# Banded attention and a mixture of experts on one core: transposes first in a step, four copies, one buffer less for h, and other work kept out of second products

## The chip, the core and the metric

The kernel runs on one core of a Trainium2 chip, as one program. The metric is the device time of one execution in microseconds (us), as the median of several runs. Before the change it is 854.83 us (three runs, 854.17 to 855.73).

## The reference

Two stages. The first is attention with a window, over 4 sequences of 576 positions and 8 heads of 64 numbers; the second sends each of the 4 · 576 = 2304 rows through all four experts and adds their outputs with normalised weights.

```python
scores = scale * np.matmul(q, k.transpose(0, 1, 3, 2))
mask_plain = (rel >= 0) & (rel < window)
mask_dil = (rel >= 0) & (rel < window * dilation) & (rel % dilation == 0)
...
attn = np.exp(scores - max); attn = attn / (attn.sum(-1) + 1e-09)
x = (attn @ v) as rows of B * S, columns of H * D        # 2304 x 512
p = domain_probs / (domain_probs.sum(-1, keepdims=True) + 1e-09)
for e in range(E):                                       # 4 experts, F = 1024
    h = np.maximum(x @ w1[e], 0.0)
    out += p[:, e:e + 1] * (h @ w2[e])
```

## The kernel before

**Precision.** Every operand of an expert's product is split in a high and a low part (ScalarE copies the high part, L113; VectorE or GpSimd subtracts it to get the low part, L116), and each product is three matmuls: high·high, low·high, high·low.

**Attention** is 48 groups of three query blocks for a pair of heads, in 25 steps of two groups (the first two steps have one). Loop pass n works on several steps at once: it issues the q·k matmuls (`s_qk`, bank `sc`, L264) and mask and maximum (`s_max`, L278, VectorE) of step n; subtraction (`s_sub`, L294, GpSimd) and exponential (`s_exp`, L302, ScalarE) of step n−1; the row sums (`s_sum`, L310, L311, VectorE) and the scaling by their inverse (`s_norm`, L317, GpSimd) of step n−2; the transposes (`s_tr`, L329, bank `pt`), with their copies to `pts` (L336 on ScalarE, L334 on VectorE), of step n−3; and the products with v (`s_av`, L349, bank `po`), with their copies into the raw x (`xr`, L365, ScalarE), of step n−4. `stages` (L371) gives the order within a pass. `sc`, `pt` and `po` share a ring of four PSUM banks. q and k come by SyncE's queue (L245, L246); v of the first two sequences is issued by ScalarE's (L252), of the others by SyncE's.

**The experts** run in visits (u, m): 256 of F's columns (u) against a block of 768 tokens (m). A visit's first product (`mm1_a`, `mm1_b`) uses a seven-product scheme after Strassen: products of six matmuls into bank x or y, and sums of them that make h. In `mm1_b` the order is S2·T2, S1·T1, S3·T3, S4·B22, A22·T4. After S1·T1 ScalarE copies y to `s5`; after S3·T3 VectorE adds x to it (L439); A22·T4 then writes x again, so it waits for that sum, with S4·B22's matmuls between. After S4·B22 VectorE adds `u2` (L443). `mm2` is the second product, two halves of three tiles, 18 matmuls a half (L480), each tile added into `acc` by VectorE (L488). The next visit's `mm1_a` (with its sum, L423) stands around the second product's halves.

**Prepared work.** Splits of weights and of x (`x_part`: low parts on GpSimd for the first half of a block, on VectorE for the second) and sums of x (`x_sums`, L203, VectorE, four of them a half block) lie in two lists, `queue` and `later`; x of blocks 1 and 2 lies in `later`. After each yield of the experts the main loop takes one piece of `queue`, and, if `queue` is short, one of `later`. `need` runs a piece to its end where it must be ready.

**The start.** In passes 0 to 9 there are only attention and dummy matmuls (`wt`, L680) on TensorE, and the fetches of the first weights: `fetch_w1(0)` in pass 3, `fetch_w2(0)` and the row weights `pw` (L737) in pass 4, `fetch_w1(1)` in pass 7. The first product comes in pass 10 (START); from pass 15 (OPEN) twelve yields of the experts go between two attention steps.

Of the kernel before, what the change touches and what calls it, by code (L numbers as in the profile page):

```python
# [8 lines left out]
F32 = mybir.dt.float32  # L9
# [7 lines left out]
KB = QB + WINDOW  # L17
GB = 3
# [24 lines left out]
def kernel(  # L43
# [12 lines left out]
    _, which = band_masks(qT.shape[3])  # L56
    B, NP, _, S = qT.shape
    NT, DM = out.shape
    E, _, F = w1.shape
# [160 lines left out]
    def attention(ap, xrp, pa):  # L220
# [14 lines left out]
        st = {}  # L235
# [11 lines left out]
            qk_t[b, p, gi] = (q_s, k_s)  # L247

        def load_v(b, p, gi):
            v_s = ap.tile([KB, 2, GB, 64], F32, tag="v", name="v_s", bufs=6)  # L250
            queue = nc.scalar if b < 2 else nc.sync
            queue.dma_start(out=v_s, in_=vw[b, p][:, :, gi * GB:(gi + 1) * GB, :])  # L252
            v_t[b, p, gi] = v_s
# [69 lines left out]
        def s_tr(n, gs):  # L323
            sm = st[n]
            outs = []
            for k in range(len(gs)):
                pt = pa.tile([128, 512], F32, tag="pa", name="pt")
                for i in range(GB):
                    nc.tensor.transpose(  # L329
                        pt[:KB, i * 128:(i + 1) * 128], sm[:, k * GB + i, :KB], ident  # L330
                    )
                ts_ = ap.tile([KB, GB * 128], F32, tag="pts", name="pts", bufs=2)
                if k and gs[k][0] > 1:
                    nc.vector.tensor_copy(ts_, pt[:KB, :GB * 128])  # L334
                else:
                    nc.scalar.activation(out=ts_, in_=pt[:KB, :GB * 128], func=AF.Copy)  # L336
                outs.append(ts_)
            st[n] = outs
# [28 lines left out]
        def load_masks():  # L367
            nc.sync.dma_start(out=mask, in_=masks)


        stages = (  # L371
            (s_sub, 1), (s_sum, 2), (s_av, 4), (s_tr, 3), (s_norm, 2), (s_exp, 1),
            (s_qk, 0), (s_max, 0),
        )
        return chunk, load_masks, load_qk, load_v, stages
# [2 lines left out]
    def product(bank, u, a, m, b_, first, last=True):  # L378
        (ah, al), (bh, bl) = a_op[u, a], x_op(m, b_)
        for k in range(2):  # L380
            for i, (w, x) in enumerate(((ah, bh), (al, bh), (ah, bl))):
                nc.tensor.matmul(  # L382
                    bank, w[:, k], x[:, k],
                    start=(first and k == 0 and i == 0), stop=(last and k == 1 and i == 2),
                    skip_group_check=True,
                )
# [3 lines left out]
    st = {}  # L390

    def bank(n):
        return pools["m1"].tile([128, 512], F32, tag=n, name=f"m1{n}")[:, :TH]

    def tmp(n):
        return fp.tile([128, TH], F32, tag=n, name=n)
# [30 lines left out]

    def mm1_b(k):
        u, m = k
        x, u2, s5 = st.pop(k), tmp("u2"), tmp("s5")  # L430
        product(x, u, "S2", m, "T2", False)
        nc.scalar.activation(out=u2, in_=x, func=AF.Copy)  # L432
        yield
        y = bank("y")
        product(y, u, "S1", m, "T1", True)
        nc.scalar.activation(out=s5, in_=y, func=AF.Copy)
        yield
        product(x, u, "S3", m, "T3", False)
        nc.vector.tensor_tensor(out=s5, in0=x, in1=s5, op=ALU.add)  # L439
        yield  # L440
        product(y, u, "S4", m, "B22", False)
        h_hi(k, "22", s5)
        nc.vector.tensor_tensor(out=u2, in0=y, in1=u2, op=ALU.add)  # L443
        h_lo(k, "22", s5)
        h_out(k, "12", u2)
        yield
        product(x, u, "A22", m, "T4", False)
        h_out(k, "21", x)
        yield
# [13 lines left out]
    def mm2(k, first, last, half):  # L463
        u, m = k
        e = u // FPE % E
        if first and m not in acc_t:
            if m == NBL - 1:
                pools["late"]()
            acc_t[m] = pools["acc"].tile([128, TB // 128, DM], F32, name=f"acc_{m}")
        for i in range(TH // 128):  # L470
            at = half * (TH // 128) + i
            tt = m * (TB // 128) + at
            acc = acc_t[m][:, at, :]
            po = pools["m2"].tile([128, 512], F32, tag="m2", name="m2")

            cs = range(2) if half == 0 else (1, 0)
            for n, (c, low) in enumerate([(c, low) for low in range(2) for c in cs]):
                h = h_t[k, f"{c + 1}{half + 1}"][low][:, i * 128:(i + 1) * 128]
                for x, w in enumerate(w2_op[u, c][:2 - low]):
                    nc.tensor.matmul(  # L480
                        po, h, w, start=(n == 0 and x == 0), stop=(n == 3)
                    )
            if first:
                nc.vector.tensor_scalar(
                    out=acc, in0=po, scalar1=pn[:, tt, e:e + 1], scalar2=None, op0=ALU.mult
                )
            else:
                nc.vector.scalar_tensor_tensor(  # L488
                    out=acc, in0=po, scalar=pn[:, tt, e:e + 1], in1=acc,
                    op0=ALU.mult, op1=ALU.add,  # L490
                )
            if last:
                nc.sync.dma_start(out=out[tt * 128:(tt + 1) * 128, :], in_=acc)
            yield


    visits = [(u, 0) for u in range(1, NU)]
# [68 lines left out]
    queue = []  # L566
    later = []

    def step(of=None):
        of = queue if of is None else of  # L570
        while of:
            if next(of[0][1], 0) != 0:
                return
            of.pop(0)
# [15 lines left out]
    with tc.manual_schedule():  # L590
# [11 lines left out]
        ap = early.enter_context(tc.tile_pool(name="attn", bufs=2, side="right"))  # L602
# [99 lines left out]
        flat = [g for s in steps for g in s]  # L702
        first_x = []
        qk_done = av_done = qk_next = v_next = 0

        dummies(18)
        ffn = experts(begin)
        for n in range(len(steps) + LAG):
            while qk_next < min(qk_done + min(6, 3 + n), len(flat)):
                load_qk(*flat[qk_next])  # L710
                if qk_next == 0:
                    load_masks()
                qk_next += 1
            while v_next < min(av_done + 6, qk_done + 2, len(flat)):
                load_v(*flat[v_next])
                v_next += 1
            for stage, lag in stages:
                if 0 <= n - lag < len(steps):
                    stage(n - lag, steps[n - lag])
            if n < len(steps):  # L720
                qk_done += len(steps[n])
            if n >= LAG:
                av_done += len(steps[n - LAG])
            for i, names in when.get(n, ()):
                for name in names:
                    of = first_x if i < 2 else later
                    if name is None or name == "T2":
                        prepare(x_sums, i, of=of)
                    if name is not None:
                        prepare(x_part, i, name.upper(), of=of)  # L730
            queue[:0] = first_x
            first_x.clear()
            if n == 3:
                fetch_w1(0)
            if n == 4:
                fetch_w2(0)
                nc.sync.dma_start(out=pw, in_=probs.rearrange("(t p) e -> p t e", p=128))  # L737
            if n == 5:
                prepare(w1_split, 0)
            if n == 7:  # L740
                prepare(w2_late, 0)
                fetch_w1(1)
            if n == START + 1:
                weigh()
                prepare(w1_split, 1)
                prepare(w1_sums, 1)
            if n == OPEN - 1:
                prepare(w2_late, 1)
            if n == START + 2:
                fetch_w2(1)  # L750
            if n == OPEN:
                fetch_w1(2)
            if n == OPEN:
                gate.add("open")
            if n < START:
                dummies(4 if n < 4 else 1)
                step()
                if n > 4:
                    step()
                    step()  # L760
                continue
            for _ in range(PACE if "open" in gate else 2):
                if next(ffn) == "idle":
                    dummies(2)
                    for _ in range(3):
                        step()
                    break
                step()
                if len(queue) > 8:
                    step()  # L770
                elif later and len(queue) < 5:
                    step(later)
        gate.add("over")
        for _ in ffn:
            step()
            if len(queue) > 6:
                step()
            step(later)


# [53 lines left out]
```

## Time and profile before

| | before |
|---|---|
| median of three runs | 854.83 us |
| the profiled execution | 850.82 us |
| its span on the core | 849.0 us |
| TensorE busy | 828.1 us (98%) |
| VectorE, ScalarE, GpSimd busy | 499.9, 327.6, 419.1 us |
| granted TensorE clock, mean | 0.994 |
| bytes moved by DMA | 56.77 MB |

The span is the time between the first and the last instruction of the core, the execution's time has some 1.8 us more around it. Busy shares are means over the whole span. "Granted clock" is the share of the full 2.4 GHz that TensorE was given; near 0.5 is its lower level, 1.2 GHz. In rows of the timeline the first two numbers are start and duration in us, and a bracket at the end gives the idle time before the instruction and what ended it; a row with x3 groups three instructions.

### The profile page before, as it was taken

Reading aid. Unit: us, or ns where it says so; the run is one execution under the profiler, and the core shown is the slowest. Engines: PE = TensorE matmul, PEld = TensorE weight load, DVE = VectorE, ACT = ScalarE, POOL = GpSimd, SP = SyncE. Lnnn points to the kernel's source line nnn. Section 1 sums busy time; section 2 is a strip of 40 time slices with the busy share of each in tenths; the row PEclk is TensorE's granted clock in tenths of the full one; section 3 lists DMA queues with packets and bytes.
Section 4 is the critical chain, followed back from the end, with each engine's and each line's share of the span. In section 5 each row is a group of like instructions: output and inputs, shape, how many; then the busy total and the mean of one; then the engine's idle time right before and its main releaser. Section 6 shows DMA issues by size and latency. Waiting matters only on the chain.

```text
span 849.0 us, 13445 instructions
## 1 busy us (share of the span) xinstructions
PE 828.1 (98%) x5090; PEld 732.1 (86%) x5090; DVE 499.9 (59%) x1027; ACT 327.6 (39%) x772; POOL 419.1 (49%) x484
## 2 busy tenths in 40 slices
PE   8798999999999999999999999999999999999998
PEld 5577788887898888899899898898998998988986
DVE  4777766669555568655545545555555455455554
ACT  3555454445454355533233233242242242232321
POOL 4677987677676678931432332342341342242210
PEclk9999999999999999999999999999999999999999
DMA  8762322332221222310100100101101001010003
GB/s 234 218 184 73 128 85 84 108 120 64 78 90 51 57 71 72 124 51 26 50 25 25 51 26 26 50 25 38 37 26 50 26 25 49 26 35 17 1 26 124
DMA packets 54528, 56.77 MB, mean 67 GB/s; under 512 B 5952, under 2 KB 43840, under 8 KB 54464
## 3 DMA queue, kind: packets, MB, share of 16 engines
q1 hardware_dynamic: 49472, 52.38, 19.9%
q10 hardware_dynamic: 4992, 3.54, 1.5%
q8 instruction: 40, 0.66, 0.3%
q14 instruction: 24, 0.20, 0.1%
HBM read 51.19 MB, written 4.72 MB: 66 GB/s over the span
## 4 chain that ended last, share of the span: by engine, by line
PE 92%; DVE 3%; DMA 1%; ACT 1%; POOL 1%; issue 1%; SPq 0%; ACTq 0%; POOLq 0%; DVEq 0%
PE m L480 45%; PE m1x L382 24%; PE m1y L382 17%; PE po L349 2%; PE sc L264 2%; PE pt L329 2%; DMA q_s<-qT 1%; PE wt L680 1%; DVE acc L488 1%; DMA k_s<-kT 1%; DVE xl_T L116 1%; DVE hl L406 0%; ACT hh L400 0%; DVE xr L203 0%; DVE s L423 0%
## 5 line engine op out<-in xcount | busy, mean ns | idle before, releaser
L488 DVE SCALAR_TENSOR_TENSOR acc<-m,pn,acc 128x512 f32<-128x512 f32 x270 | 201.9, 749 | 130.9 <-PE m L480 130.7
L480 PE MATMUL m<-w2h,hh 128*128 128x512 f32 x576 | 226.9, 394 | 3.9 <-DVE acc L488 3.2
L480 PE MATMUL m<-w2l,hh 128*128 128x512 f32 x576 | 225.4, 391 | 0.0
L116 POOL TENSOR_TENSOR g2l<-r,g2h 128x256 fp32r<-128x256 f32 x124 | 93.0, 775 | 239.7 <-PE m L480 212.2
L480 PE MATMUL m<-w2h,hl 128*128 128x512 f32 x576 | 178.5, 391 | 0.0
L400 ACT ACTIVATE hh<-s 128x384 fp32r<-128x384 f32 x94 | 49.4, 526 | 248.3 <-DVE s L423 197.8
L480 PEld LDWEIGHTS m<-w2h,hh 128*128 128x128 f32 x576 | 108.1, 188 | 26.8 <-DVE acc L488 6.1
L480 PEld LDWEIGHTS m<-w2h,hl 128*128 128x128 f32 x576 | 108.1, 188 | 24.0 <-DVE hl L406 0.3
L480 PEld LDWEIGHTS m<-w2l,hh 128*128 128x128 f32 x576 | 108.2, 188 | 20.1
L116 POOL TENSOR_TENSOR w2l<-r,w2h 128x512 fp32r<-128x512 f32 x62 | 80.6, 1320 | 45.4 <-ACT w2h L113 45.0
L116 POOL TENSOR_TENSOR g1l<-r,g1h 128x256 fp32r<-128x256 f32 x93 | 68.5, 752 | 66.9 <-ACT g1h L113 66.9
L439 DVE TENSOR_TENSOR s<-m1x,s 128x384 f32<-128x384 f32 x47 | 26.2, 557 | 103.0 <-PE m1x L382 101.3
L432 ACT ACTIVATE u<-m1x 128x384 f32<-128x384 f32 x47 | 23.1, 492 | 144.4 <-PE m1x L382 144.4
L406 DVE SCALAR_TENSOR_TENSOR hl<-s,hh 128x384 fp32r<-128x384 f32 x94 | 60.2, 640 | 28.4 <-ACT hh L400 28.4
L382 PE MATMUL m1x<-xh_T,g2h 128*128 128x384 f32 x156 | 53.1, 340 | 1.8 <-DVE s L423 1.8
L382 PE MATMUL m1x<-xl_T,g2h 128*128 128x384 f32 x156 | 52.9, 339 | 0.0
L382 PE MATMUL m1x<-xh_T,g2l 128*128 128x384 f32 x156 | 52.7, 338 | 0.0
L113 ACT ACTIVATE g2h<-r 128x256 fp32r<-128x256 f32 x125 | 43.4, 405 | 4.4 <-POOL r L145 4.4
L382 PE MATMUL m1y<-xl_B,g2h 128*128 128x384 f32 x128 | 43.0, 336 | 0.0
L382 PE MATMUL m1y<-xh_B,g2h 128*128 128x384 f32 x128 | 43.0, 336 | 0.0
L382 PE MATMUL m1y<-xh_B,g2l 128*128 128x384 f32 x128 | 42.9, 335 | 0.0
L278 DVE CUSTOM_DVE_ANT_0 sm<-sc,mask 128x96 f32<-128x96 f32 x144 | 27.8, 254 | 18.8 <-PE sc L264 17.4
(92 smaller groups left out, 1542.3 us busy)
## 6 DMA issues: line engine op xcount, KB each, us to landing
r<-w SPq DMA_DIRECT2D x64, 512.0 KB, 3.5
k_s<-kT SPq DMA_DIRECT2D x48, 112.0 KB, 3.3
q_s<-qT SPq DMA_DIRECT2D x48, 96.0 KB, 3.4
out<-acc SPq DMA_DIRECT2D x18, 256.0 KB, 2.0
v_s<-vw ACTq DMA_DIRECT2D x24, 144.0 KB, 4.1
v_s<-vw SPq DMA_DIRECT2D x24, 144.0 KB, 3.2
mask<-masks SPq DMA_DIRECT2D x1, 288.0 KB, 4.6
pw<-probs SPq DMA_DIRECT2D x1, 36.0 KB, 5.9
```

Of the source, the lines that this page charges most:

```text
L113: nc.scalar.activation(out=hi, in_=src, func=AF.Copy)
L116: lo_eng.tensor_tensor(out=lo, in0=src, in1=hi.bitcast(F32), op=ALU.subtract)
L264: nc.tensor.matmul(banks[swap][o, i * KB:(i + 1) * KB], q_s[h, c0:c0 + QB], k_s[h, c0:c0 + KB], start=True, stop=True, skip_group_check=True,)
L278: nc.vector.tensor_tensor_reduce(out=sm[:, k * GB + i, :KB], in0=banks[k][:, i * KB:(i + 1) * KB], in1=mask[:, which[blk if p < NP // 2 el ...
L329: nc.tensor.transpose(pt[:KB, i * 128:(i + 1) * 128], sm[:, k * GB + i, :KB], ident)
L382: nc.tensor.matmul(bank, w[:, k], x[:, k], start=(first and k == 0 and i == 0), stop=(last and k == 1 and i == 2), skip_group_check=True,)
L400: nc.scalar.activation(out=hi, in_=src, func=AF.Relu)
L406: nc.vector.scalar_tensor_tensor(out=lo, in0=src, scalar=0.0, in1=hi.bitcast(F32), op0=ALU.max, op1=ALU.subtract)
L432: nc.scalar.activation(out=u2, in_=x, func=AF.Copy)
L439: nc.vector.tensor_tensor(out=s5, in0=x, in1=s5, op=ALU.add)
L480: nc.tensor.matmul(po, h, w, start=(n == 0 and x == 0), stop=(n == 3))
L488: nc.vector.scalar_tensor_tensor(out=acc, in0=po, scalar=pn[:, tt, e:e + 1], in1=acc, op0=ALU.mult, op1=ALU.add,)
```

## The change

1. In a pass `s_tr` comes before `s_av`, and `pts` has four buffers instead of two.
2. `s5` takes the buffer of `s1` (tag "s1") instead of its own; `v_s` has five buffers instead of six.
3. Pieces of `later` are taken only after yields of the first products (`mm2` now yields "acc"), and with fewer than 8 pieces in `queue` instead of fewer than 5.
4. q and k are loaded six groups ahead from the first pass on, instead of 3 + n at first.
5. `fetch_w2(0)` and `pw` move from pass 4 to pass 6, `w2_late(0)` and `fetch_w1(1)` from pass 7 to pass 8.

```diff
--- before.py
+++ after.py
@@ -247,7 +247,7 @@
             qk_t[b, p, gi] = (q_s, k_s)
 
         def load_v(b, p, gi):
-            v_s = ap.tile([KB, 2, GB, 64], F32, tag="v", name="v_s", bufs=6)
+            v_s = ap.tile([KB, 2, GB, 64], F32, tag="v", name="v_s", bufs=5)
             queue = nc.scalar if b < 2 else nc.sync
             queue.dma_start(out=v_s, in_=vw[b, p][:, :, gi * GB:(gi + 1) * GB, :])
             v_t[b, p, gi] = v_s
@@ -329,7 +329,7 @@
                     nc.tensor.transpose(
                         pt[:KB, i * 128:(i + 1) * 128], sm[:, k * GB + i, :KB], ident
                     )
-                ts_ = ap.tile([KB, GB * 128], F32, tag="pts", name="pts", bufs=2)
+                ts_ = ap.tile([KB, GB * 128], F32, tag="pts", name="pts", bufs=4)
                 if k and gs[k][0] > 1:
                     nc.vector.tensor_copy(ts_, pt[:KB, :GB * 128])
                 else:
@@ -369,7 +369,7 @@
 
 
         stages = (
-            (s_sub, 1), (s_sum, 2), (s_av, 4), (s_tr, 3), (s_norm, 2), (s_exp, 1),
+            (s_sub, 1), (s_sum, 2), (s_tr, 3), (s_av, 4), (s_norm, 2), (s_exp, 1),
             (s_qk, 0), (s_max, 0),
         )
         return chunk, load_masks, load_qk, load_v, stages
@@ -427,7 +427,7 @@
 
     def mm1_b(k):
         u, m = k
-        x, u2, s5 = st.pop(k), tmp("u2"), tmp("s5")
+        x, u2, s5 = st.pop(k), tmp("u2"), tmp("s1")
         product(x, u, "S2", m, "T2", False)
         nc.scalar.activation(out=u2, in_=x, func=AF.Copy)
         yield
@@ -491,7 +491,7 @@
                 )
             if last:
                 nc.sync.dma_start(out=out[tt * 128:(tt + 1) * 128, :], in_=acc)
-            yield
+            yield "acc"
 
 
     visits = [(u, 0) for u in range(1, NU)]
@@ -706,12 +706,12 @@
         dummies(18)
         ffn = experts(begin)
         for n in range(len(steps) + LAG):
-            while qk_next < min(qk_done + min(6, 3 + n), len(flat)):
+            while qk_next < min(qk_done + 6, len(flat)):
                 load_qk(*flat[qk_next])
                 if qk_next == 0:
                     load_masks()
                 qk_next += 1
-            while v_next < min(av_done + 6, qk_done + 2, len(flat)):
+            while v_next < min(av_done + 5, qk_done + 2, len(flat)):
                 load_v(*flat[v_next])
                 v_next += 1
             for stage, lag in stages:
@@ -732,12 +732,12 @@
             first_x.clear()
             if n == 3:
                 fetch_w1(0)
-            if n == 4:
+            if n == 6:
                 fetch_w2(0)
                 nc.sync.dma_start(out=pw, in_=probs.rearrange("(t p) e -> p t e", p=128))
             if n == 5:
                 prepare(w1_split, 0)
-            if n == 7:
+            if n == 8:
                 prepare(w2_late, 0)
                 fetch_w1(1)
             if n == START + 1:
@@ -760,7 +760,8 @@
                     step()
                 continue
             for _ in range(PACE if "open" in gate else 2):
-                if next(ffn) == "idle":
+                at = next(ffn)
+                if at == "idle":
                     dummies(2)
                     for _ in range(3):
                         step()
@@ -768,14 +769,16 @@
                 step()
                 if len(queue) > 8:
                     step()
-                elif later and len(queue) < 5:
+                elif at != "acc" and len(queue) < 8:
+
                     step(later)
         gate.add("over")
-        for _ in ffn:
+        for at in ffn:
             step()
             if len(queue) > 6:
                 step()
-            step(later)
+            if at != "acc":
+                step(later)
 
 
 # ---- launch: one core ----
```

Three places of the new order. SyncE's queue first, around the first w2 (`r` of L106) and `pw`; the row of L98 is the fetch of the first w1. Before:

```order
L98 DMA r_299<-w 128x4x256
L245 DMA q_s<-qT 128x192
L246 DMA k_s<-kT 128x224
L245 DMA q_s<-qT 128x192
L246 DMA k_s<-kT 128x224
L106 DMA r_360<-w 128x2x512
L737 DMA pw<-probs 128x18x4
L245 DMA q_s<-qT 128x192
L246 DMA k_s<-kT 128x224
```

With the change, the last of the loads ahead of w2:

```order
L245 DMA q_s<-qT 128x192
L246 DMA k_s<-kT 128x224
L245 DMA q_s<-qT 128x192
L246 DMA k_s<-kT 128x224
L245 DMA q_s<-qT 128x192
L246 DMA k_s<-kT 128x224
L106 DMA r_493<-w 128x2x512
L737 DMA pw<-probs 128x18x4
L245 DMA q_s<-qT 128x192
L246 DMA k_s<-kT 128x224
```

Between the first w1 and w2 stood the q and k of two groups, and now of six; the rows ahead of that w1 are in the order that they had. The second w1 moves back by two groups.

ScalarE in passes 5 and 6, `v_s` being the issue of a transfer. Before:

```order
L113 ACTIVATE g1h<-r_299 128x256 x3
L252 DMA v_s<-vw 96x2x192
L365 ACTIVATE xr<-po 128x4x48 x2
L336 ACTIVATE pts<-pt 96x384 x2
L302 ACTIVATE sm_96<-sm_96 128x6x96
L113 ACTIVATE g2h<-r_299 128x2x128
L252 DMA v_s<-vw 96x2x192 x2
L365 ACTIVATE xr<-po 128x4x48 x2
```

With the change:

```order
L113 ACTIVATE g1h<-r_297 128x256 x3
L252 DMA v_s<-vw 96x2x192
L336 ACTIVATE pts<-pt 96x384 x2
L365 ACTIVATE xr<-po 128x4x48 x2
L302 ACTIVATE sm_96<-sm_96 128x6x96
L113 ACTIVATE g2h<-r_297 128x2x128
L252 DMA v_s<-vw 96x2x192 x2
L336 ACTIVATE pts<-pt 96x384 x2
```

The copies `pts` of the transposes come ahead of the copies `xr` of the products with v; the transfers keep their places. On TensorE the `pt` rows stand ahead of the `po` rows in the same way.

VectorE in the middle of the attention, at a visit's first product, where block 1's second half of x is split (`xl_B_1`). Before:

```order
L488 SCALAR_TENSOR_TENSOR acc_983<-m_2734,pn,acc_983 128x512
L116 TENSOR_TENSOR xl_B_1_1478<-xr,xh_B_1_1477 128x2x192
L488 SCALAR_TENSOR_TENSOR acc_983<-m_2746,pn,acc_983 128x512
L116 TENSOR_TENSOR xl_B_1_1493<-xr,xh_B_1_1492 128x2x192
L488 SCALAR_TENSOR_TENSOR acc_983<-m_2758,pn,acc_983 128x512
L116 TENSOR_TENSOR xl_B_1_1528<-xr,xh_B_1_1527 128x2x192
L203 TENSOR_TENSOR xr<-xr 128x2x192 x2
L439 TENSOR_TENSOR s_2775<-m1x,s_2775 128x384
L203 TENSOR_TENSOR xr<-xr 128x2x192
L443 TENSOR_TENSOR u_2774<-m1y,u_2774 128x384
```

With the change:

```order
L488 SCALAR_TENSOR_TENSOR acc_981<-m_2732,pn,acc_981 128x512
L488 SCALAR_TENSOR_TENSOR acc_981<-m_2742,pn,acc_981 128x512
L488 SCALAR_TENSOR_TENSOR acc_981<-m_2752,pn,acc_981 128x512
L116 TENSOR_TENSOR xl_B_1_1476<-xr,xh_B_1_1475 128x2x192
L116 TENSOR_TENSOR xl_B_1_1491<-xr,xh_B_1_1490 128x2x192
L439 TENSOR_TENSOR s_2767<-m1x,s_2767 128x384
L116 TENSOR_TENSOR xl_B_1_1505<-xr,xh_B_1_1504 128x2x192
L443 TENSOR_TENSOR u_2766<-m1y,u_2766 128x384
L406 SCALAR_TENSOR_TENSOR hl<-s_2767,hh 128x384
L406 SCALAR_TENSOR_TENSOR hl<-u_2766,hh 128x384
```

The splits leave the places between the sums into `acc`; two now stand ahead of the sum of L439 and one ahead of that of L443.

## Rows read from the trace of the kernel before

**Rows 1.** Head of the page: the span and its instructions

```profile
span 849.0 us, 13445 instructions
```

**Rows 2.** Stretches: us, busy (instructions) PE, PEld, DVE, ACT, POOL, PEclk, DMA share, GB/s

```profile
0.00:40.00 40.00, 31.32 (x462) 21.91 (x465) 23.28 (x132) 18.86 (x46) 21.35 (x29) 0.91 0.82 226
78.80:82.20 3.40, 3.40 (x13) 3.00 (x11) 2.10 (x2) 2.68 (x7) 3.40 (x4) 0.53 0.50 152
304.57:305.61 1.04, 1.04 (x7) 1.04 (x7) 0.84 (x2) 0.60 (x2) 0.96 (x2) 1.00 0.00 0
306.66:310.79 4.13, 4.13 (x20) 3.39 (x20) 2.67 (x4) 1.83 (x4) 4.01 (x5) 1.00 0.00 0
340.00:849.00 509.00, 505.11 (x2521) 456.18 (x2519) 269.53 (x426) 161.85 (x370) 169.53 (x206) 1.00 0.12 40
```

**Rows 3.** TensorE's waits: for what, us in total, times, longest us

```profile
PE pt L329 <- POOL sm L317: 4.5, 3, 2.0
PE m L480 <- DVE acc L488: 3.2, 2, 1.9
PE sc L264 <- ACT xr L365: 2.6, 2, 1.4
```

**Rows 4.** The chain to the first product, start us, us, what

```profile
31.42 4.84 DMA k_s<-kT
36.30 0.33 ACT xr L365
...
37.04 0.71 PE sc L264 x20
...
40.33 1.27 PE m1x L382 x6
```

**Rows 5.** Timeline of SyncE's queue: start us, us, engine, line, operation

```profile
17.49 0.47 SPq L737 DMA_DIRECT2D pw<-probs  x1
18.93 3.61 SPq L245 DMA_DIRECT2D q_s<-qT  x1
```

**Rows 6.** Timeline, all engines, 20 to 26 us, one wait of the transposes

```profile
20.74 2.04 DVE L116 TENSOR_TENSOR g1l<-r,g1h 128x256 fp32r<-128x256 f32 x3
...
23.82 1.15 POOL L317 TENSOR_TENSOR sm<-sm,rc 128x576 f32<-128x576 f32 x1 [1.65 <-DVE rc L311]
...
25.02 0.86 PE L329 MATMUL pt<-ident,sm 128*96 128x128 f32 x6 [1.78 <-POOL sm L317]
```

**Rows 7.** Timeline, 59 to 63 us, another such wait

```profile
59.74 0.92 PE L349 MATMUL po<-pts,v_s 96*64 96x64 f32 x24
...
62.67 0.75 PE L329 MATMUL pt<-ident,sm 128*96 128x128 f32 x5 [2.00 <-POOL sm L317]
```

**Rows 8.** Timeline, 96 to 98 us, inside a second product

```profile
96.10 1.07 DVE L203 TENSOR_TENSOR xr<-xr 128x384 f32<-128x384 f32 x1
...
97.89 0.50 PE L480 MATMUL m<-w2h,hh 128*128 128x512 f32 x1 [1.89 <-DVE acc L488]
```

**Rows 9.** Timeline, 205 and 210 us: VectorE's split and what TensorE then waits for

```profile
205.51 1.52 DVE L116 TENSOR_TENSOR xl_T<-xr,xh_T 128x384 fp32r<-128x384 f32 x1
...
211.75 0.50 PE L480 MATMUL m<-w2h,hh 128*128 128x512 f32 x1 [1.27 <-DVE acc L488]
```

**Rows 10.** Timeline, 319 to 321 us: a split ahead of a first product's sum

```profile
319.63 0.67 DVE L116 TENSOR_TENSOR xl_B<-xr,xh_B 128x384 fp32r<-128x384 f32 x1 [2.03 <-ACT xh_B L113]
...
320.22 0.55 DVE L439 TENSOR_TENSOR s<-m1x,s 128x384 f32<-128x384 f32 x1
...
320.82 0.44 PE L382 MATMUL m1x<-xh_T,g1h 128*128 128x384 f32 x1 [0.50 <-DVE s L439]
```

**Rows 11.** VectorE by line and form: busy us, mean ns, idle before

```profile
L203 DVE TENSOR_TENSOR xr<-xr 128x384 f32<-128x384 f32 x24 | 19.0, 794 | 0.1
...
L116 DVE TENSOR_TENSOR xl_T<-xr,xh_T 128x384 fp32r<-128x384 f32 x11 | 11.2, 1022 | 2.9 <-ACT xh_T L113 2.8
...
L116 DVE TENSOR_TENSOR w2l<-r,w2h 128x512 fp32r<-128x512 f32 x2 | 2.4, 1199 | 0.0
```

## The prediction

> **What bounds the kernel now.** I read the head of the page first, then the table of stretches, then TensorE's list of waits, then the chain, and only then the timeline at the places that these name. The span is 849.0 us [rows 1]; the execution with what lies around the span took 850.82 us, and the median of the three runs is 854.83 us, 4.0 us above it. I work out a difference against the profiled execution and add it to the median. In the long stretch from 340 us on TensorE is busy 505.11 of 509 us and DMA at 0.12 of its share [rows 2]: nothing that the change does there can give or take more than single waits. Up to 40 us it is another kernel: TensorE is filled up with dummies, and DMA runs at 0.82 of its share with 226 GB/s, so the transfers decide when the first product can begin. The list of waits [rows 3] gives the places in between: 4.5 us for the scaling by the row sums (three times), 3.2 us for sums into acc (twice), 2.6 us for the copies of x (twice, both before 40 us). All the waits that the change can take away are together about 10 us, and a part of them lies under dummies.
>
> **The start, moved transfers.** The chain to the first product says what is last there [rows 4]: a load of k issued at 31.42 lands 4.84 us later, at 36.26; ScalarE, whose queue stood behind the issue of a v load, makes its copies of x at 36.30; the q·k matmuls that need the bank follow at 37.04; the first product is at 40.33. The second w1, 128 x 4 x 256 fp32 = 0.52 MB, stands ahead of that k and is moved behind it. At 226 GB/s [rows 2] it is worth 0.52 / 226 = 2.3 us. Taking it away is a gain of 2.3 us if everything behind it moves up. Against that: `pw` goes out in pieces of 16 bytes; the load of q behind it took 3.61 us to issue [rows 5]. The change does not remove this, it moves it two passes nearer to the first product, and the w2 ahead of it too. The two low parts of w2 on VectorE, 1.20 us each [rows 11], now come in one step, ahead of the row sums of a step that the first product waits for. What that does is seen with three g1l splits of 2.04 us: the scaling by the sums comes at 23.82 and the transposes wait 1.78 us [rows 6]. With 2.4 us of splits in place of 2.04 I count 1.6 us back. So −2.3 + 1.6 = **−0.7 us**. Bounds: −3.5, if the 2.3 us are kept and one wait of 1.2 us for copies of x goes with them (half of 2.6 for two); +1.5, if nothing is gained and the split costs its 1.6. That q and k are loaded six ahead from the first pass changes no row of SyncE's queue up to the first w1, so I cost it at nothing.
>
> **Transposes first.** In pass n the transposes wait for GpSimd's scaling of the pass before. So far the products with v, 0.92 us [rows 7], were issued ahead of them and covered the tail of that scaling; now they come behind. At the second wait shown, the products begin at 59.74 and the transposes at 62.67 after 2.00 us idle [rows 7]; with the transposes first the idle time is 2.92, and nothing is taken from the products behind them: they only move. TensorE works in order, so what follows in this pass comes 0.92 us later. I take **+0.9 us** for this one; of the other two waits in the list both are before 40 us and under the first term. Bounds 0 (the slack is caught up by the sums behind) and +1.8 (one more pass so). What the order gives, that the copies to `pts` are there long before they are used, hides a wait of 1.8 us at the very start only, where the transfers decide anyway. Four `pts` in place of two are needed for it and cost nothing; one v buffer less lets the issue of v come one group later, and the transfer waits longest in the start, under the first term.
>
> **One buffer for s1 and s5.** ScalarE's copy to s1 now waits for the low part made of s5, one product earlier. It is issued during the second product's half, 4.13 us long [rows 2], so it is hidden; if that low part came over 3 us late, it would show. **0.**
>
> **Work out of the second product.** At 96.10 a subtraction of 1.07 us stands ahead of a sum into acc, and TensorE waits 1.89 us [rows 8]. In the new order a subtraction that stood ahead of the first product's sum goes behind, but one still stands ahead of the first acc; later ones go. I take **−0.6 us** (0 to −1.9). At 205.51 a split of 1.52 us holds up the next sums, and TensorE waits 1.27 us before 211.75 [rows 9]; this wait goes wholly. But the splits come back in the first products, where there is less room: after S3·T3 the sum into s5 has one product, 1.04 us [rows 2], before TensorE needs bank x. At 319.63 one split of 0.67 us stood just ahead of that sum, which ended at 320.77, and TensorE lost 0.50 us [rows 10]. In the changed order there are two places with two splits ahead of the sum. Each split needs ScalarE's high part first, so it cannot start before the product in which it is issued is nearly over. I count 0.6 us for the first place (splits of B, as at 319.63), 1.5 us for the second (splits of T, mean 1.02 us [rows 11], up to 1.52 [rows 9], the second starting where S3·T3 is half done), and 0.8 us for the low parts behind the further splits; together 2.9, less the 1.3 that goes: **+1.6 us**. Bounds −1.3 (the splits fit in) and +3.5, if all the splits in the four visits take 1.52.
>
> How a split comes to last 1.52 us, when others take 0.67, is weighed best by the rows: GpSimd is busy 4.01 of 4.13 us in a stretch of this kind [rows 2], and the longer durations are where it works. The Trainium skill, "GPSIMD Engine Reference", section "Specifications", says that GpSimd's interfaces to SBUF are shared with VectorE, for instructions of VectorE with two SBUF inputs among others; a split has two. By this rule every split in a first product beside GpSimd's weight splits would take the long duration, and the term would be at +3.5 instead of +1.6. The rows show both durations, so I stay between.
>
> **Seven subtractions together.** For the last block of x, seven subtractions of x now stand in one lump ahead of the sums of a second product's half: 7 · 0.794 = 5.6 us [rows 11]. Behind them come three sums into acc, 0.74 us each, and the sum into s5, 0.55 [rows 10]: 8.4 us, begun about 1 us into the half. TensorE has the half, 4.13 us, and four products, 4 · 1.04, together 8.3 us, before it needs that sum. So it waits about 1.1 us, and with subtractions of 1.07 us [rows 8] 3.0. The 0.50 us of before [rows 10] belongs to the same block. I take 1.6 − 0.5 = **+1.1 us** (−0.5 to +2.5).
>
> **Sum.** −0.7 + 0.9 + 0 − 0.6 + 1.6 + 1.1 = +2.3 us. On the profiled execution 853.1, on the median 857.1 us. About 0.2%, 1.7 us, is what a measurement of this kernel can tell from no change; the sum lies just above it.
>
> **The rivals.** *Faster.* The transfers in the start decide, and the w1 that is moved away brings its 2.3 us in full, since the split of w2 finds idle VectorE time (23.28 of 40 us busy [rows 2]); the splits of x fit in the first products. Then −2.3 + 0.9 − 0.6 − 1.3 − 0.5 = −3.8 us: 851.0. It decides from the point where the row sums behind w2's splits are not late. For it speaks the chain [rows 4], against it the 1.78 us of [rows 6]. *No difference.* The start gains 2.3 and the splits cost what I count: −2.3 + 0.9 − 0.6 + 1.6 + 1.1 = +0.7, or 855.5. *Slower by the clock.* After waits TensorE has been at 0.53 of its clock for 3.40 us and did 13 matmuls [rows 2], where at full clock six take 1.04: 3.4 − 13 · 0.174 = 1.1 us lost. If the longer waits that I forecast bring two or three such stretches, 2.3 + 2 · 1.1 = +4.5: 859.3. The Trainium skill, "TensorE: Matmul & The Clock Gate", Part 1, says that idle time takes the clock back to 1.2 GHz; no row shows it for waits of under 1 us. *Slower by long splits.* GpSimd is busy throughout the first products in question and every split there lasts 1.52 us [rows 9]: 2.3 − 1.6 + 3.5 = +4.2, or 859.0. Against it speaks the 0.67 us at 319.63 [rows 10]. This is the case that the page on GpSimd makes likely. *The change does not do what it says:* the order of the loads at the start stays as it was up to w1, so that part does nothing; it is in the sum as zero.
>
> **Chances.** My forecast 0.28, slower by the clock 0.07, slower by long splits 0.06, no difference 0.25, faster 0.34. So faster 0.34, within 0.2% 0.25, slower 0.41. The range goes from 849.8 (the faster case with a little more at the start) to 861.0 (the clock's case with a larger term of the splits); the forecast's own is 856.5 to 858.5.
>
> **What would show it.** Right: a first product at 39 to 40 us; the wait for the scaling near 60 us at about 2.9; no wait for acc near 210; waits for the sums of L439 near 205, 220 and in the block after 320, of 0.6, 1.5 and 1.6 us. Wrong: a first product before 38.5, or no wait for L439 over 0.5 us, means the faster case; a TensorE clock at half after 40 us more often than once, the clock's.

## The result: slower by 9.2 us, four times the forecast

The changed kernel takes 864.46 us (median of 6 runs, 862.34 to 866.32), the one before 855.28 us (6 runs, 853.98 to 856.06). The ratio is 1.011, with a 95% interval from 1.0094 to 1.0126: 8.0 to 10.8 us slower. The direction is the one forecast, the size is not: 857.1 us was forecast, and 861.0 was the upper end of the range.

The profiled execution took 864.04 us, next to its median; that of before, 850.82, lies below all six of its own runs, so the two traces differ by 13 us where the medians differ by 9. The head of the page of the changed kernel:

```profile
span 862.2 us, 13393 instructions
...
PE 833.6 (97%) x5090; PEld 738.9 (86%) x5090; DVE 500.6 (58%) x1027; ACT 326.3 (38%) x772; POOL 417.5 (48%) x484
```

The list of TensorE's waits (for what, us in total, times, longest):

```profile
PE pt L329 <- POOL sm L317: 9.5, 7, 3.1
PE m L480 <- DVE acc L488: 4.7, 3, 2.3
PE m1x L382 <- DVE s L439: 4.7, 3, 3.4
PE m1x L382 <- DVE s L423: 1.8, 1, 1.8
```

Against [rows 3] the transposes' wait has gone from 4.5 us to 9.5, that for acc from 3.2 to 4.7, and that for the sum of L439 from the 0.50 of [rows 10] to 4.7, with one wait of 3.4. The waits for copies of x, 2.6 us, are gone from it. The stretches with TensorE alone (us, busy, PEclk, DMA share, GB/s):

```profile
0.00:40.00 40.00, 30.98 (x442) 0.88 0.85 228
40.90:44.00 3.10, 3.10 (x24) 0.50 0.45 93
64.30:71.70 7.40, 6.49 (x62) 0.54 0.46 136
85.00:88.70 3.70, 3.70 (x16) 0.54 0.44 142
211.40:214.60 3.20, 3.20 (x20) 0.50 0.63 221
340.00:849.00 509.00, 505.58 (x2531) 1.00 0.12 39
```

Four stretches after 40 us are at the lower clock, where [rows 2] have one. From 340 us on TensorE is idle for 3.4 us, which is one wait; behind it the two traces run side by side, 13.0 us apart, to the end. The first product moved little; the last of the chain that leads to it (start us, us):

```profile
36.10 1.16 POOL sm L317
37.30 1.51 PE pt L329 x6
...
40.30 1.17 PE sc L264 x24
41.47 2.22 PE m1x L382 x6
```

It comes at 41.47 instead of 40.33 [rows 4], no longer behind a load of k but behind GpSimd's scaling, and its six matmuls take 2.22 us instead of 1.27.

When the first matmul of each run of first and second products in the two traces is set side by side, the 13 us arise in four places: 2.1 us up to 50 us, 3.9 between there and 75 us, 4.2 between 205 and 230 us, and 3.7 at 350 us, less about 1 us in between. The first two lie where the transposes wait and where the clock is low; this is the wait of the second:

```profile
65.21 1.09 PE L329 MATMUL pt<-ident,sm 128*96 128x128 f32 x4 [3.07 <-POOL sm L317]
```

The last two are these. At 210 us:

```profile
205.53 1.09 DVE L203 TENSOR_TENSOR xr<-xr 128x384 f32<-128x384 f32 x1
...
206.61 2.83 POOL L116 TENSOR_TENSOR w2l<-r,w2h 128x512 fp32r<-128x512 f32 x2 [0.40 <-ACT w2h L113]
...
207.01 2.84 DVE L203 TENSOR_TENSOR xr<-xr 128x384 f32<-128x384 f32 x2
...
209.77 1.40 DVE L488 SCALAR_TENSOR_TENSOR acc<-m,pn,acc 128x512 f32<-128x512 f32 x2
...
210.56 0.50 PE L480 MATMUL m<-w2h,hh 128*128 128x512 f32 x1 [2.32 <-DVE acc L488]
```

Three subtractions, the first and the other two with one row of L406 (a low part of h) between them, stand ahead of the sums into acc, and TensorE waits 2.32 us. Around it stand three shorter waits, two for the sum of L439 and one more for acc:

```profile
203.10 0.45 PE L382 MATMUL m1x<-xh_T,g1h 128*128 128x384 f32 x1 [0.62 <-DVE s L439]
...
220.75 0.50 PE L480 MATMUL m<-w2h,hh 128*128 128x512 f32 x1 [0.79 <-DVE acc L488]
...
227.21 0.44 PE L382 MATMUL m1x<-xh_T,g1h 128*128 128x384 f32 x1 [0.62 <-DVE s L439]
```

From 205 us on the waits are 2.32, 0.79 and 0.62, together 3.73 us, where before had the 1.27 of [rows 9]; the rest of the 4.2 us has the size of what the stretch at low clock from 211.40 on can cost. At 349 us:

```profile
339.79 7.14 DVE L203 TENSOR_TENSOR xr<-xr 128x384 f32<-128x384 f32 x7
...
346.85 2.06 DVE L488 SCALAR_TENSOR_TENSOR acc<-m,pn,acc 128x512 f32<-128x512 f32 x3
...
348.83 0.54 DVE L439 TENSOR_TENSOR s<-m1x,s 128x384 f32<-128x384 f32 x1
...
349.43 0.45 PE L382 MATMUL m1x<-xh_T,g1h 128*128 128x384 f32 x1 [3.42 <-DVE s L439]
```

The lump of seven holds up three sums into acc and then the sum into s5, and TensorE waits 3.42 us.

### The profile page after: what moved, and what is told of

Read it like the earlier page. It is cut to its first block, busy times and chain, and to the rows that moved or that the text cites. A ratio compares the mean times of both kernels' runs of the same rounds, so it can differ in the third digit from the quotient of the medians.

```text
span 862.2 us, 13393 instructions
## 1 busy us (share of the span) xinstructions
PE 833.6 (97%) x5090; PEld 738.9 (86%) x5090; DVE 500.6 (58%) x1027; ACT 326.3 (38%) x772; POOL 417.5 (48%) x484
## 4 chain that ended last, share of the span: by engine, by line
PE 90%; DVE 4%; POOL 2%; ACT 1%; DMA 1%; issue 1%; ACTq 0%; SPq 0%; DVEq 0%; POOLq 0%
PE m L480 44%; PE m1x L382 23%; PE m1y L382 17%; PE po L349 2%; PE pt L329 2%; PE sc L264 1%; DVE xr L203 1%; DMA q_s<-qT 1%; DVE acc L488 1%; POOL sm L317 1%; DVE hl L406 1%; DMA k_s<-kT 1%; ACT hh L400 0%; DVE s L423 0%; DVE sm L278 0%
## 5 line engine op out<-in xcount | busy, mean ns | idle before, releaser
L439 DVE TENSOR_TENSOR s<-m1x,s 128x384 f32<-128x384 f32 x47 | 26.2, 557 | 100.1 <-PE m1x L382 98.4
L406 DVE SCALAR_TENSOR_TENSOR hl<-s,hh 128x384 fp32r<-128x384 f32 x94 | 59.6, 635 | 27.9 <-ACT hh L400 27.8
```

Of the source, the lines that this page charges most:

```text
L406: nc.vector.scalar_tensor_tensor(out=lo, in0=src, scalar=0.0, in1=hi.bitcast(F32), op0=ALU.max, op1=ALU.subtract)
```

## The experiments

Each ratio is against the kernel before on the same chip, as it is on record (not exactly the quotient of the two medians), with its 95% interval; 0.001 is 0.86 us.

### The four parts, one at a time

**Order**, with the edits of the small parts (below), which make room for the four copies:

```diff
-            (s_sub, 1), (s_sum, 2), (s_av, 4), (s_tr, 3), (s_norm, 2), (s_exp, 1),
+            (s_sub, 1), (s_sum, 2), (s_tr, 3), (s_av, 4), (s_norm, 2), (s_exp, 1),
...
-                ts_ = ap.tile([KB, GB * 128], F32, tag="pts", name="pts", bufs=2)
+                ts_ = ap.tile([KB, GB * 128], F32, tag="pts", name="pts", bufs=4)
```

> The kernel before with the transposes first, four copies, and what makes room for them (one buffer for s1 and s5, five of v, six groups of q and k ahead); transfers and the rule for the other blocks' x stay as before. Theory 'wait plus clock': transposes first let TensorE stand idle for the whole of GpSimd's scaling in one piece, so the wait near 62 us grows from 2.00 to about 3.0 us and TensorE's clock falls to 1.2 GHz for some 7 us behind it; the time is 3 to 5 us above before. Rival 'transfers': the order costs only the 0.9 us of the longer wait and the rest of the loss comes from the moved loads; within 1 us of before.

Measured 1.0006 (0.9992 to 1.0021), +0.5 us: the theory's 3 to 5 us are not there, though its profile has what the theory described, a wait of 3.1 us and a stretch at low clock behind it:

```profile
PE pt L329 <- POOL sm L317: 8.1, 6, 3.1
```

```profile
62.20:69.80 7.60, 7.00 (x64) 6.25 (x65) 5.44 (x19) 3.09 (x8) 2.80 (x3) 0.55 0.48 134
```

The first is from the list of waits, the second from the table of stretches, as [rows 2]. What the theory missed is that the order of before has a stretch at low clock here too, in most profiles: the next runs show it, 3.4 us long. It was the profile of before that had none (columns as in [rows 2]):

```profile
62.00:70.00 8.00, 6.75 (x58) 6.01 (x59) 6.99 (x22) 4.64 (x13) 3.34 (x4) 1.00 0.46 126
```

What the transposes first do change is its length, about 7 us in all three profiles that have them first and no dummies there. In the median no more than a little of this shows: beside the run of the small parts, which this one contains, it is 1.2 us slower, and each of the two is known to about 1.2 us.

**The rule for the other blocks' x** (the change's point 3 alone, both loops):

```diff
-                elif later and len(queue) < 5:
+                elif at != "acc" and len(queue) < 8:
                     step(later)
...
-            step(later)
+            if at != "acc":
+                step(later)
```

> The kernel before with only the rule that the other blocks' x is taken at first products. Theory 'wait plus clock': the waits near 205 to 216 us (subtractions beside sums into acc, 2.3 us, and a stretch at half clock) and the lump of seven subtractions (3.4 us in place of 0.5) are this part's alone: 6 to 8 us above before, less some 1 us of waits that go. Rival 'the parts act on each other': the wait near 205 us comes only with the other order of a pass and the lump costs 3 us; 2 to 3 us above before.

Measured 1.0089 (1.006 to 1.0118), +7.6 us. The rule is most of the loss. Its trace has both waits that the theory named, with the clock low behind the second and not behind the first (the last row is of the table of stretches):

```profile
205.29 0.50 PE L480 MATMUL m<-w2h,hh 128*128 128x512 f32 x1 [2.32 <-DVE acc L488]
...
342.39 0.69 PE L382 MATMUL m1x<-xh_T,g1h 128*128 128x384 f32 x1 [3.46 <-DVE s L439]
```

```profile
341.20:348.40 7.20, 6.01 (x18) 5.59 (x19) 3.74 (x8) 3.60 (x9) 2.12 (x4) 0.53 0.01 2
```

**Later fetches** (point 5 alone):

```diff
-            if n == 4:
+            if n == 6:
                 fetch_w2(0)
...
-            if n == 7:
+            if n == 8:
                 prepare(w2_late, 0)
```

> The kernel before with only w2, the row weights and the second w1 fetched later. Theory 'wait plus clock': the first product comes at 39 to 40.5 us, as before within 1 us, and the time is within 1 us of before. Rival 'transfers': two low parts of w2 on VectorE in one pass make the first product 1 to 2 us late, and the time is 1 to 3 us above before.

Measured 0.9991 (0.9976 to 1.0006), −0.8 us: no loss in the moved loads, though this execution's first product came at 42.13 us on the timeline, where that of before stands at 40.26, 1.9 us after it and outside what the theory expected.

**The small parts** (s5 in s1's buffer, five of v, six groups ahead):

```diff
-        x, u2, s5 = st.pop(k), tmp("u2"), tmp("s5")
+        x, u2, s5 = st.pop(k), tmp("u2"), tmp("s1")
...
-            while qk_next < min(qk_done + min(6, 3 + n), len(flat)):
+            while qk_next < min(qk_done + 6, len(flat)):
...
-            while v_next < min(av_done + 6, qk_done + 2, len(flat)):
+            while v_next < min(av_done + 5, qk_done + 2, len(flat)):
```

> The kernel before with only one buffer for s1 and s5, five buffers of v and q and k six ahead. Both theories: nothing but the first pass' wait on ScalarE (1.8 us near 12 us) changes; within 1 us of before.

Measured 0.9992 (0.9978 to 1.0007), −0.7 us: nothing that can be told. Its profile, with transposes last as before, shows the low clock behind the same wait, here of 2.38 us and ended at 64.28:

```profile
65.30:68.70 3.40, 3.40 (x32) 3.18 (x27) 3.37 (x18) 1.12 (x3) 1.01 (x2) 0.51 0.66 220
```

### The rule in two halves, and the change without it

After the attention only, which brings the lump (the second piece of the diff of the rule):

> The kernel before with the rule only for the time after the attention (the loop over what is left of the experts). One lump of seven subtractions, nothing else moved before it. Theory 'later': the lump makes the sum into s5 of the next visit late by 3.4 us in place of 0.5, so some 3 us, and up to 3 more where the clock is low after it: 3 to 6 us above before. Rival 'spread': most of the loss of the rule lies near 205 us, and the lump alone costs under 1.5 us.

Measured 1.0053 (1.0034 to 1.0071), +4.5 us. Its timeline has the change's lump and the change's wait, 7.6 us earlier:

```profile
332.20 7.15 DVE L203 TENSOR_TENSOR xr<-xr 128x384 f32<-128x384 f32 x7
...
341.85 0.69 PE L382 MATMUL m1x<-xh_T,g1h 128*128 128x384 f32 x1 [3.42 <-DVE s L439]
```

and, in this execution, the low clock behind it (columns as in [rows 2]):

```profile
341.20:345.00 3.80, 3.15 (x10) 3.16 (x11) 2.33 (x6) 1.76 (x4) 0.34 (x1) 0.56 0.00 0
```

The wait is 2.9 us longer than the 0.50 of [rows 10]. The changed kernel's own profile has the wait without such a stretch. Set side by side with the trace of before as above, this one falls behind by another 1.6 us after the wait, that of the whole rule by 2.7, and that of the changed kernel by 0.1. So a stretch at low clock follows the lump in two of three profiles, and it can make up what the wait leaves of the 4.5 us; how often it comes was not counted.

During the attention only (the first piece of that diff):

> The kernel before with the rule only during the attention. Theory 'later': a wait of 2.3 us for acc near 205 to 211 us in place of 1.3 near 210, two of 0.6 for the sum into s5, and one of 0.8 near 220, less 0.9 near 97: 1.5 to 3.5 us above before. Rival 'spread': 5 us or more above before.

Measured 1.0043 (1.0027 to 1.006), +3.7 us, just above the 1.5 to 3.5 expected. In its trace the 2.32 us for acc are there, at 210 us, with the clock at 1.00 behind them, and two new waits for the sum of L439 of 0.6 us; against the profile of before, some 3.5 us arise between 195 and 220 us:

```profile
PE m L480 <- DVE acc L488: 4.6, 3, 2.3
...
PE m1x L382 <- DVE s L439: 1.7, 3, 0.6
```

The change with both pieces of that diff taken back:

> The changed kernel with the rule for the other blocks' x taken back, all else as changed. Theory 'later': the rule is nearly all of the loss; within 1.5 us of before (854 to 857). Rival 'parts act on each other': transposes first together with the later w2 make the start late by what neither does alone; 2 to 3 us above before.

Measured 1.0015 (0.9999 to 1.0031), +1.3 us. The halves and this add up, 4.5 + 3.7 + 1.3 = 9.5 us, to the 9.2 of the whole; each of the three is known to about 1.5 us.

### The lump taken apart

```diff
             if at != "acc":
                 step(later)
+                step(later)
```

on the run with the lump: the subtractions come as 2, 2 and 4, and earlier.

> The kernel before with the rule only for the time after the attention, but two pieces of the other block's x at each first product's yield, so that the subtractions come as 2, 2 and 4 instead of 1 and 7, and half a visit earlier. Theory 'a lump that ends behind its due time': the wait of 3.4 us for the sum into s5 goes; within 1 us of before, and 3 us or more below the run with the lump. Rival 'VectorE's subtractions beside first products cost wherever they stand': 2 to 4 us above before.

Measured 1.0033 (1.0014 to 1.0051), +2.8 us: the rival's size. The wait of 3.4 us is gone; in its place there are one for the sum of L439, behind splits, and one for acc, behind the four subtractions:

```profile
325.83 0.45 PE L382 MATMUL m1x<-xh_T,g1h 128*128 128x384 f32 x1 [1.14 <-DVE s L439]
...
336.68 0.50 PE L480 MATMUL m<-w2h,hh 128*128 128x512 f32 x1 [1.31 <-DVE acc L488]
```

In these places the subtractions are not free either.

### The clock

24 more dummy matmuls in pass 14, on the change without the rule:

```diff
-                    dummies(2)
+                    dummies(26 if n == OPEN - 1 else 2)
```

> The same as the run without the rule, with 24 more dummy matmuls on TensorE in pass 14, ahead of the transposes that wait for GpSimd's scaling near 62 us. If the idle time itself takes the clock down, the stretch at half clock behind it (62 to 70 us) goes, and the time is 1.5 to 3 us below the run without dummies. If the clock falls whatever TensorE does there, or if that stretch is hidden by other waits: within 1 us of it.

The run without them and the run with them (table of stretches):

```profile
63.40:70.00 6.60, 5.62 (x59) 4.87 (x60) 4.57 (x18) 3.47 (x8) 3.18 (x3) 0.50 0.61 173
```

```profile
62.00:72.00 10.00, 10.00 (x122) 7.82 (x121) 6.68 (x31) 4.04 (x10) 6.19 (x7) 1.00 0.46 132
```

The stretch is gone: it was TensorE standing idle that brought the clock down there. The four profiles of kernels with more dummies in pass 14 (this run and the three runs with dummies below) have no such stretch, eight of the ten without have one. Side by side the trace with dummies gains 1.9 us on the other between 51 and 71 us. In time the two are 1.0015 and 1.0003 of before, 1.0 us apart, less than the two intervals can tell; the 26 dummies took 4.29 us, longer than the wait of 3.07 that they filled.

The same on the kernel before, with 18 more in pass 14 and with 16 ahead of the first S2·T2:

```diff
             need_x(m)
+            if i == 0:
+                dummies(16)
             yield from mm1_b((u, m))
```

> The kernel before with 18 more dummy matmuls in pass 14 (ahead of the transposes that wait near 62 us) and 16 ahead of the first S2·T2 (which waits 1.84 us near 76 us for the sum of L423). Theory 'idle time takes the clock down': the stretches at half clock behind these two places (65 to 69 and 79 to 83 us) go, the waits themselves stay; 1.5 to 3 us below before. Rival: the dummies cost what the clock gives, or the clock falls at a later wait in their place; within 1 us of before.

Measured 0.999 (0.997 to 1.001). In its trace the clock is 1.00 at both places; the time is −0.9 us, no difference that can be told. With the later fetches added:

> The kernel before with the same dummies and with w2, the row weights and the second w1 fetched later as in the change. If the two act apart: the sum of both, 2 to 4 us below before. If the later w2 only moves waits about the start: as the run with the dummies alone.

Measured 0.9982 (0.9962 to 1.0002), −1.5 us, nearly a gain. Its profile had the start at low clock for 13 us:

```profile
30.40:43.60 13.20, 11.02 (x131) 8.58 (x132) 7.35 (x34) 8.21 (x21) 6.54 (x6) 0.50 0.73 206
```

So the last run fills the start too:

```diff
-                dummies(4 if n < 4 else 1)
+                dummies(4 if n < 4 else 8)
```

> The run with dummies and later fetches, and 8 dummy matmuls instead of 1 in each of the passes 4 to 9, ahead of the first product. If the transfers set the pace of the start and TensorE has room there, the low clock that lay over the first product (30 to 44 us) goes, and the time is 1 to 2 us below that run, 3 to 4 us below before, faster than both kernels. If TensorE has no room there, the six times 0.75 us of dummies make the first product late and the time is 1 to 4 us above that run.

Measured 852.77 us, 0.9978 (0.9964 to 0.9991): 1.9 us faster than before, and so faster than both kernels, though not the 3 to 4 us expected, and no further from the run before it than the intervals allow. The 1.9 us are those of the dummies at two places, the later fetches and the filled start together; none of the three was told from nothing by itself. Its trace is at full clock from 20.7 us on:

```profile
20.70:44.00 23.30, 21.67 (x346) 15.96 (x345) 18.09 (x91) 15.78 (x40) 15.12 (x13) 1.00 0.79 211
```

## Why the prediction was right in sign and wrong in size

The step that failed is the price of the work on x that the rule moves: −0.6, +1.6 and +1.1 us, together +2.1, where the run of the rule alone measured +7.6 (5.1 to 10.1). The two halves of it failed in different ways.

**"Seven subtractions together", +1.1 us: measured +4.5 (2.9 to 6.1).** The mechanism was the one named, and the term was mis-sized at both its ends. The subtractions took 7.14 us, 1.02 each, and not the 5.6 of the mean of [rows 11]; that mean is over short ones and ones of 1.07 us [rows 8], and here GpSimd was splitting or adding weights beside all of them. And the lump began 2.1 us after the product ahead of the half had ended, not 1, since the sum of L423, the high part on ScalarE and the low part come first. Both together make 2.6 us late, added to the 1.1 forecast 3.7; the wait was 3.42. The bound of +2.5 was too low for the same reason. Less the 0.50 of before the wait is 2.9 of the 4.5 us; what is left has the size of the low clock behind it, which this term did not hold and the clock's rival did.

**"Work out of the second product", −0.6 and +1.6, +1.0 us together: measured +3.7 (2.3 to 5.1).** Here a step was missed. I priced the splits ahead of L439, two places with 0.6 and 1.5 us; the trace has 0.62 and 0.62. The wait of 1.89 us [rows 8], of which I took 0.6 as gained, is still there with 1.60. I did not price the three subtractions that the same rule put ahead of the sums of a second product's half, although the rule counts pieces at first products and these land behind them, in front of acc. That is the wait of 2.32 us at 210.56, where I had written that there would be none, and the one of 0.79 at 220.75. The 3.2 us at half clock behind the first stand in the profile of the changed kernel alone: the two runs with the same wait, of the whole rule and of its part during the attention, have none there.

What stands beside the long subtractions is the thing that I weighed and then halved. At 205 to 210 us two subtractions take 2.84 us, 1.42 each, while GpSimd takes 2.83 for two weight splits; with GpSimd idle, one takes 0.55:

```profile
50.70 0.55 DVE L203 TENSOR_TENSOR xr<-xr 128x384 f32<-128x384 f32 x1
```

The Trainium skill, "GPSIMD Engine Reference", "Specifications", says that GpSimd and VectorE contend for the same interfaces where VectorE has two SBUF inputs. The trace agrees: 1.42 us in place of 0.55 at 207.01, and 1.02 in the lump. Of the 24 subtractions of this form in the changed kernel's trace, the nine with GpSimd idle take 0.54 to 0.56 us, and the fifteen with GpSimd at work beside them 0.90 to 1.50. It is not so every time: in the trace of before two take 0.54 and 0.55 with GpSimd busy beside most of each. No run took GpSimd's work away, so this is read from the traces and not shown by an experiment. The case "slower by long splits", at 859.0, was the nearest of the rivals in its mechanism, but it was worked out for the splits and not for the subtractions, which have two such inputs as well.

**"Transposes first", +0.9, and "the start", −0.7.** The run of the order, which has the small parts with it, gave +0.5 (−0.7 to +1.8), that of the fetches −0.8 (−2.1 to +0.5): each in reach of its term, and neither told from nothing, so that neither mechanism is shown in the median. The wait near 62 us grew from 2.00 to 3.07, by the 0.92 forecast and a little. All but the rule together were +1.3 (−0.1 to +2.7). The first product at 41.47 us was out of the 39 to 40 forecast, but this number cannot judge the term (below). The reading under the term is open too: in the trace of before ScalarE's issue of two loads of v runs from 34.99 to 36.25 us, so the copies at 36.30 [rows 4] may have waited for that and not for the load of k that landed at 36.26.

**The clock.** The rival that brought the time of the clock in by two or three stretches was right that they come: four after 40 us, where the profile of before has one. But the comparison was with a single execution. Of the six other kernels that have the transposes last and no dummies there, five show a stretch of 3.4 us between 65 and 70 us in their profiles. That a stretch stands there is therefore not new with the change; that it is twice as long with the transposes first is, in three profiles of three. I put 1.1 us on 3.4 us at half clock [rows 2]; the traces with the lump fall behind by 1.6 us with one such stretch behind it and by 2.7 with one twice as long. What the stretch near 65 us is worth in the median was not settled by the runs with dummies.

**That q and k six ahead do nothing** was right as far as the run of the small parts can tell.

## What to carry to other kernels

Price a moved instruction by what it has beside it in the new place, not by its mean: here the mean was 0.79 us, and the lump paid 1.02, seven times. A rule that says where a piece of work may be taken must be followed to what happens when it is not taken in time: the rest is forced out in one lump, at the latest place there is. And a single profile of a kernel whose executions differ by 0.5 to 0.9% (the kernel before, beside the experiments) is one draw: before a difference in a stretch is explained, see whether another profile of the same instructions has it.

## What the runs showed that was not expected

Up to the first product, the kernel before and five of the experiments (the rule, its halves, two pieces each, the dummies on before) issue the same instructions. Their first products came at 40.26, 39.95, 41.15, 43.38, 42.08 and 42.55 us: 3.4 us apart, with low-clock stretches in the first 45 us that differ in place and length. The forecast for the start, −0.7 us, is a fifth of that, so the first product of one profile cannot judge it.

Dummy matmuls that fill the start, eight in each of six passes, did no harm that shows, although eight take TensorE 1.37 us in the trace, where the one of the run before took 0.28: the first product came at 42.19 us, and at 43.15 in that run.
